# Who empties the first keys' bank, and when, in the first steps of an attention and feed-forward kernel

## The chip, the cores and the metric

One core of a Trainium2 chip runs one program. TensorE (PE) multiplies and transposes, VectorE (DVE) and ScalarE (ACT) work on what it leaves in its accumulator banks, GpSimd (POOL) works on on-chip memory, and SyncE (SP) issues the transfers. The metric is the device time of one execution in microseconds, as the median of several runs.

## The reference

Three blocks in a row: causal attention with a cumulative bias, a gated feed-forward block, and a mixing block.

```python
def _attn_ref(q, k, v, s):                       # (4, 8, 576, 64), s: (4, 8, 576)
    scores = (1 / np.sqrt(D)) * np.matmul(q, k.transpose(0, 1, 3, 2))
    cum = np.cumsum(np.maximum(s, 0.0), axis=-1)
    bias = -(cum[:, :, :, None] - cum[:, :, None, :])
    scores = np.where(causal, -1000000000.0, scores + np.minimum(bias, 0.0))
    scores = scores - np.max(scores, axis=-1, keepdims=True)
    attn = np.exp(scores)
    attn = attn / (np.sum(attn, axis=-1, keepdims=True) + 1e-09)
    return np.matmul(attn, v)
def _moe_ref(x, w_in, g_ln, w_sg, b_sg, w_out):  # x: (4, 576, 512)
    u, v = halves of gelu(x @ w_in)
    v_s = np.einsum('ts,bsd->btd', w_sg, layernorm(v) * g_ln) + b_sg[None, :, None]
    return x + (u * v_s) @ w_out
def _moe2_ref(x, w_theta, w_tok_r, w_tok_i, w_ch):
    theta = x @ w_theta
    u = x + einsum(w_tok_r, x * cos(theta)) + einsum(w_tok_i, x * sin(theta))
    return u + np.maximum(u @ w_ch, 0.0)
```

## The kernel before

**Tiling.** Attention is done for 16 pairs of heads (4 batches of 4 pairs), each pair stacked to 128 partitions. A pair's 576 queries are five tiles `t` = 0 to 4, and a tile's causal row of exponentials is 64, 192, 320, 448 or 576 keys wide. The exponentials of both heads (`j` = 0, 1) lie in one tile `E`. For the value product they must be turned, keys onto partitions: 128x128 transposes (L465) write them to accumulator banks `T`, and an eviction brings each bank to on-chip memory. The banks have four kinds. Kind a holds the last keys (two blocks of one head, and for the second head also the 64 first keys of tile 0), kind b four blocks that go to `Ef[:, 512:1024]`, kind c four that go to `Ef[:, 0:512]`, and kind d the four blocks of the *first keys* of both heads, which go to `E0[:, 0:512]`. Kinds a and c are emptied by ScalarE (L477, L481, L483), kinds b and d by VectorE (L475, L479).

**The value product** (`values`) accumulates in two banks, Y and Z. Its calls are in this order: two over E0 (the first keys), two over `Ef` 0:512, two of 384 columns, two of 128, two of 256 columns over the last keys, and two over the 64 first keys of tile 0 into Z. VectorE multiplies the result by the reciprocal sums (L536, L537) and `finish_pair` makes the high and low halves `x` for the feed-forward block. The reciprocal sums `r` of a pair are turned by one transpose (`turned`, L490) into a part of a bank, copied to `rT` by ScalarE (L492), stored, and loaded again, spread over partitions, as `xT` (`load_r`, L509).

**Banks.** Scores use four accumulator banks. A pool of two banks holds Y, Z and, outside the cases below, every T; a second pool of two holds the feed-forward accumulators `fo` and, in the first steps, the banks of kinds b and d and that of the sums' transpose. A bank is written again only when its eviction has been done.

**Order.** Attention begins with hand-written steps p = 1 to 4 (`first_steps`, `FIXED` = 5), whose instructions stand on each engine in the order in which they are written. Step p does, for pair p: scores of tiles 4, 1, 0, then of 3, 2; `reduced` (VectorE, L424: bias, mask and the row's extreme); `expo` (ScalarE, L435: exponentials and their sums); `inverse` (VectorE, L440 and L441: the reciprocals). In the same step it does the value product of pair p-2, with the sums' transpose of pair g = p-1 in its midst (the argument `between` of `values`), and the transposes of pair g, whose evictions are written between the reductions and exponentials. Beside these, VectorE, ScalarE and POOL prepare a feed-forward weight (`bits`: L744, L745, L749; `part32`: the cast to `wih` at L104 and the low half `wil` at L112).

After step 4 come the value product of pair 3 and the loop of `attention`, p = 5 to 16. There scores, transposes (`transpose_units`) and value products of three pairs are units of a string, and between units feed-forward products fill TensorE by a plan; a scheduler then sets the order of the instructions. `transpose_units` gives the kinds in the order c0, b0, a0, c1, b1, a1, d.

Of the kernel before, what the change touches and what calls it, by code (L numbers as in the profile page):

```python
# [55 lines left out]
class Kernel:  # L56
# [396 lines left out]
    def transposes(self, pr, kind, j, pool=None):  # L453

        nc = self.nc
        E, E0 = self.Es[pr], self.E0[pr % 2]
        blocks = {"a": [(0, 3, 3), (128, 4, 3)] + ([(256, 0, 0)] if j else []),
                  "b": [(QS[t] - 192, t, 2) for t in range(2, 5)] + [(384, 4, 4)],
                  "c": [(QS[t] - 64, t, 1) for t in range(1, 5)],
                  "d": [(QS[t] - 64, t, 0) for t in range(1, 5)]}[kind]  # L460
        T = self.psF.tile([P, 512], F32, name="T", tag="fo") if pool else self.psT.tile(
            [P, 512], F32, name="T", tag="T")
        for col, t, kt in blocks:
            c = EOFF[t] + QE[t] - 64 if kt == 0 else EOFF[t] + (QE[t] + QS[kt] if j else QE[t] - QE[kt])
            nc.tensor.transpose(T[:, col:col + P], E[:, c:c + P], self.ident)  # L465
        if kind == "a" and not j and not pool and pr not in self.turns:
            self.turned(pr, T)
        if kind != "d":
            Ef = self.Efs.get((pr, j))
            if Ef is None:  # L470
                Ef = self.Efs[pr, j] = self.a2.tile([P, 1280], F32, name="Ef", tag="Ef", bufs=3)

        def away():
            if kind == "b":
                nc.vector.tensor_copy(Ef[:, 512:1024], T)  # L475
            elif kind == "c":
                nc.scalar.copy(Ef[:, 0:512], T)  # L477
            elif kind == "d":
                nc.vector.tensor_copy(E0[:, 0:512], T)  # L479
            else:  # L480
                nc.scalar.copy(Ef[:, 1024:1280], T[:, 0:256])  # L481
                if j:
                    nc.scalar.copy(E0[:, 512:576], T[:, 256:320])  # L483
        return away
# [12 lines left out]
        self.ET[pr] = (self.E0[pr % 2], [self.Efs.pop((pr, j)) for j in (0, 1)])  # L497

    def transpose_units(self, pr):
        for kind, j, cost in (("c", 0, 440.0), ("b", 0, 440.0), ("a", 0, 330.0), ("c", 1, 440.0),  # L500
                              ("b", 1, 440.0), ("a", 1, 330.0), ("d", 1, 440.0)):
            self.transposes(pr, kind, j)()
            yield cost
        self.transposed(pr)
# [6 lines left out]
    def values(self, pr, between=None):  # L511

        nc = self.nc
        E0, Efs = self.ET.pop(pr)
        v0, vr = self.vop.pop(pr)
        Y = self.psT.tile([P, 512], F32, name="Y", tag="T")
        Z = self.psT.tile([P, 512], F32, name="Z", tag="T")[:, 0:64]

        calls = []
        halves = [slice(i * D, i * D + D) for i in (0, 1)]  # L520
        for js in halves:
            calls.append((Y[js], v0[:, js], E0[:, 0:512], True, False))
        for kt, a, c, n in ((1, 0, 0, 512), (2, 128, 512, 384), (4, 384, 896, 128), (3, 256, 1024, 256)):
            for js, F in zip(halves, Efs):
                calls.append((Y[js, a:a + n], vr[:, kt - 1, js], F[:, c:c + n], False, kt == 3))
        for js in halves:
            calls.append((Z[js], v0[:, js], E0[:, 512:576], True, True))
        if between:
            self.row(calls[0:4])
            between()  # L530
            calls = calls[4:]
        self.row(calls)

        def away(eng="act"):
            xT = self.xTs.pop(pr)
            nc.vector.tensor_tensor(xT[:, 512:576], Z, xT[:, 512:576], op=ALU.mult)  # L536
            nc.vector.tensor_tensor(xT[:, 0:512], Y, xT[:, 0:512], op=ALU.mult)  # L537
            self.finish_pair(pr, xT, eng)
        return away
# [41 lines left out]
    def first_steps(self):  # L581

        self.load_cum(1)
        self.load_piece(1)
        self.load_v(0)
        self.scale(0)
        self.scores(0, 1)
        self.spin(self.psT.tile([P, 512], F32, name="spin", tag="T"), 8)
        for t in (3, 2):
            self.reduced(0, (t,))  # L590
            self.expo(0, (t,))
        del self.cums[0]
        self.bits(0)
        self.inverse(0)
        self.high(2)
        self.scale(1)

        room = self.f1.tile([P, 5 * FH], F32, name="room", tag="vT")
        self.load_cum(2)
        self.load_pair(3, at=room[:, 0:2 * S])  # L600
        for p in range(1, self.FIXED):
            g = p - 1
            self.scores(p, 0)
            if p == 1:
                self.turned(g, self.psF.tile([P, 512], F32, name="T", tag="fo"))
                self.load_pair(4, "K")
                self.load_piece(2)
            else:
                self.load_cum(p + 1)
                self.load_piece(p + 1)  # L610
                if p == 2:
                    self.load_pair(5, at=room[:, 2 * S:4 * S])
                elif p == 3:
                    self.load_pair(6, "K")
            self.reduced(p, (1, 0, 4), (0,))
            if p == 1:
                self.expo(p, (1, 0, 4), (0,))
                a0 = self.transposes(g, "a", 0)
                c0 = self.transposes(g, "c", 0)
                b0 = self.transposes(g, "b", 0, True)  # L620
                self.part32(g)
                self.reduced(p, (1, 0, 4), (1,))
                a0()
                c0()
                self.expo(p, (1, 0, 4), (1,))
                b0()
                self.load_r(g)
                self.scores(p, 1)
            else:
                self.scale(p)  # L630
                away = self.values(
                    p - 2, lambda: self.turned(g, self.psF.tile([P, 512], F32, name="T", tag="fo")))
                self.part32(g)
                self.expo(p, (1, 0, 4), (0,))
                self.reduced(p, (1, 0, 4), (1,))
                self.expo(p, (1, 0, 4), (1,))
                self.low_q(p + 1, self.raw.pop(("Q", p + 1)))
                if p == 3:
                    self.load_pair(6, "Q")
                self.scores(p, 1)  # L640
                away("pool")
                self.load_r(g)
                self.load_v(p)
                a0 = self.transposes(g, "a", 0)
                b0 = self.transposes(g, "b", 0, True)
                c0 = self.transposes(g, "c", 0)
            b1 = self.transposes(g, "b", 1, True)
            self.reduced(p, (3,))
            if p == 1:
                self.expo(p, (3,))  # L650
                self.low_q(p + 1, self.raw.pop(("Q", p + 1)))
                self.load_pair(4, "Q")
                self.load_v(p)
            else:
                a0()
                self.expo(p, (3,), (0,))
                c0()
                self.expo(p, (3,), (1,))
                b0()
            if p + 2 <= self.FIXED:  # L660
                self.high(p + 2)
            a1 = self.transposes(g, "a", 1)
            a1()
            self.reduced(p, (2,))
            del self.cums[p]
            d = self.transposes(g, "d", 1, True)
            c1 = self.transposes(g, "c", 1)
            if p < self.FIXED - 1:
                self.expo(p, (2,), (0,))
                c1()  # L670
            else:
                c1()
                self.expo(p, (2,), (0,))
            self.expo(p, (2,), (1,))
            b1()
            d()
            self.transposed(g)
            if p < self.FIXED - 1:
                self.bits(p, lambda: self.inverse(p))
            else:  # L680
                self.inverse(p)
                self.bits(p)
                self.load_piece(p + 2)
        self.part32(self.FIXED - 1)
        queued = next(i for i in reversed(self.nc.cur_bb.bb.instructions) if i.engine == mybir.EngineType.SP)
        self.values(self.FIXED - 2)("act")
        return queued
# [688 lines left out]
```

## Time and profile before

| | before |
|---|---|
| median of 3 runs | 635.86 us (635.04 to 636.33) |
| profiled execution | 635.9 us, of which span 634.2 us |
| TensorE's granted clock in it | 0.999 of full speed |
| TensorE busy | 98% of the span |
| VectorE / ScalarE / POOL busy | 68% / 55% / 27% |

A row of a timeline gives the start in us from the span's start, the length in us, the engine, the line, the operation with its output and input, the count of such instructions, and in square brackets the idle time before it with what released it. Neighbouring instructions overlap, so an engine goes on a little before the length of a row is over. The kernel counts its steps from 1; step 3 lies at 34.58 to 45.08 us by TensorE's scores, step 4 at 45.08 to 56.

### The profile page before, as it was taken

The numbers are of one execution on the slowest core, as the hardware profiler recorded it, in microseconds if no ns is written. First come the engines' busy times: TensorE is split into PE (matmuls) and PEld (weight loads), VectorE is DVE, ScalarE is ACT, GpSimd is POOL, SyncE is SP. The second block draws the span as 40 slices with busy tenths as digits, with TensorE's granted clock in tenths as the row PEclk, the third lists the DMA queues.
The fourth block names the chain that finished last, engine by engine and source line by source line (L and its number), as shares of the span: only waits on it lengthen the run. The fifth ranks groups of instructions, "written<-read, shape, count | busy, mean of one in ns | idle before, by whom it ended". The sixth has DMA issues, their size and how long they took to land.

```text
span 634.2 us, 12664 instructions
## 1 busy us (share of the span) xinstructions
PE 618.7 (98%) x4703; PEld 542.1 (85%) x4703; DVE 429.6 (68%) x1051; ACT 348.6 (55%) x808; POOL 172.2 (27%) x199
## 2 busy tenths in 40 slices
PE   8999998999999999999999999999999999999997
PEld 6676777887787788778799998899999899999997
DVE  7898678556787786888386367878654674578222
ACT  6886788756779555884265145646432561465000
POOL 6464524433043431134446554000001000100000
PEclk9999999999999999999999999999999999999999
DMA  6876772776564756336468696320013001200101
GB/s 186 273 241 209 234 214 83 221 232 224 163 186 155 244 201 199 115 93 227 161 212 250 201 328 220 111 77 20 1 38 114 1 1 57 94 0 2 75 1 75
DMA packets 54878, 90.98 MB, mean 143 GB/s; under 512 B 8640, under 2 KB 22560, under 8 KB 54816
## 3 DMA queue, kind: packets, MB, share of 16 engines
q1 hardware_dynamic: 54816, 90.17, 44.2%
q8 instruction: 37, 0.61, 0.4%
q14 instruction: 25, 0.20, 0.1%
HBM read 65.32 MB, written 24.83 MB: 142 GB/s over the span
## 4 chain that ended last, share of the span: by engine, by line
PE 67%; DVE 6%; ACT 4%; DMA 3%; POOL 2%; issue 1%; SPq 0%; DVEq 0%; ACTq 0%; POOLq 0%
PE yo L115 18%; PE fo L115 18%; PE co L115 8%; PE th L115 7%; PE wo L115 5%; PE Y L115 4%; PE T L465 3%; PE sc L115 3%; DMA x2d<-xr 1%; POOL vT L941 1%; PE tp L1092 1%; ACT E L435 1%; DMA wd<-wtabs 1%; DMA x2T<-x2d 1%; DVE stats L1015 1%
## 5 line engine op out<-in xcount | busy, mean ns | idle before, releaser
L435 ACT ACTIVATE E<-E,negm 128x192 f32<-128x192 f32 (+4 forms) x160 | 88.3, 554 | 6.3 <-DVE negm L424 6.0
L115 PE MATMUL yo<-wkl,zh 128*128 128x288 f32 x288 | 85.5, 297 | 0.0
L115 PE MATMUL yo<-wkh,zl 128*128 128x288 f32 x288 | 85.4, 297 | 0.0
L115 PE MATMUL yo<-wkh,zh 128*128 128x288 f32 x288 | 84.8, 296 | 0.0
L424 DVE CUSTOM_DVE_ANT_0 E<-sc,C 128x192 f32<-128x192 f32 (+4 forms) x160 | 69.0, 485 | 2.6 <-PE sc L115 1.8
L465 PE MATMUL T<-ident,E 128*128 128x128 f32 x400 | 57.0, 276 | 3.2 <-DVE xT L537 1.2
L115 PE MATMUL fo<-x,wih 128*128 128x288 f32 x256 | 56.3, 303 | 1.9 <-ACT uT L1012 1.9
L115 PEld LDWEIGHTS yo<-wkl,zh 128*128 128x128 f32 x288 | 54.1, 188 | 0.6
L115 PEld LDWEIGHTS yo<-wkh,zh 128*128 128x128 f32 x288 | 53.9, 188 | 0.5
L115 PEld LDWEIGHTS yo<-wkh,zl 128*128 128x128 f32 x288 | 54.0, 188 | 0.4
L465 PEld LDWEIGHTS T<-ident,E 128*128 128x128 f32 x400 | 45.7, 140 | 7.5 <-DVE Ef L475 2.1
L115 PEld LDWEIGHTS fo<-x,wih 128*128 128x128 f32 x256 | 41.8, 188 | 4.8 <-ACT uT L1012 3.0
L108 POOL TENSOR_SCALAR xt<-x2s 128x128 fp32r<-128x128 f32 x8 | 4.0, 494 | 148.7 <-DVE x2s L112 147.9
L115 PE MATMUL fo<-wih,x 128*128 128x512 f32 x128 | 42.7, 403 | 0.0
L115 PE MATMUL sc<-kh,qh 64*128 64x288 f32 (+1 forms) x192 | 39.1, 365 | 1.4 <-DVE negm L424 1.1
L1049 POOL TENSOR_TENSOR uT<-gt,uT 128x288 f32<-128x288 f32 x32 | 26.4, 830 | 51.7 <-DVE gt L1047 45.3
L115 PE MATMUL fo<-wsh,vh 128*128 128x288 f32 x128 | 38.7, 306 | 1.0 <-DVE gt L1047 1.0
L115 PE MATMUL wo<-gh,woh 128*128 128x288 f32 x128 | 38.3, 300 | 0.4 <-DVE xr L1068 0.4
L115 PE MATMUL fo<-x,wil 128*128 128x288 f32 x128 | 38.4, 303 | 0.0
L115 PE MATMUL Y<-Ef,vr 128*64 128x512 f32 (+3 forms) x256 | 38.1, 434 | 0.0
L115 PE MATMUL fo<-wsl,vh 128*128 128x288 f32 x128 | 37.9, 299 | 0.0
L115 PE MATMUL fo<-wsh,vl 128*128 128x288 f32 x128 | 37.8, 298 | 0.0
(228 smaller groups left out, 1763.5 us busy)
## 6 DMA issues: line engine op xcount, KB each, us to landing
C<-cd SPq DMA_DIRECT2D x15, 576.0 KB, 5.3
xT<-rd SPq DMA_DIRECT2D x32, 144.0 KB, 3.3
xd<-xT SPq DMA_DIRECT2D x16, 288.0 KB, 4.9
gd<-uT SPq DMA_DIRECT2D x16, 288.0 KB, 3.0
gr<-gd SPq DMA_DIRECT2D x16, 288.0 KB, 4.5
xr<-xd SPq DMA_DIRECT2D x16, 288.0 KB, 4.5
x2d<-xr SPq DMA_DIRECT2D x16, 288.0 KB, 2.5
x2T<-x2d SPq DMA_DIRECT2D x16, 288.0 KB, 4.1
```

The costliest lines, as they stand in the source:

```text
L108: nc.gpsimd.tensor_scalar(out, src, 1.0, 1.0, op0=ALU.mult, op1=ALU.mult)
L115: return self.nc.tensor.matmul(out, lhsT, rhs, start=start, stop=stop)
L424: self.nc.vector.tensor_tensor_reduce(at if j else at[:, ::-1], self.sc[t, j].rearrange("p (b k) -> p b k", k=64), C[:, j, 0:n].rearrange( ...
L435: self.nc.scalar.activation(at, at, AF.Exp, bias=self.negm[pr % 2][:, j, c:c + 1], scale=-1.0, accum_out=sm[:, j * 5 + c:j * 5 + c + 1])
L465: nc.tensor.transpose(T[:, col:col + P], E[:, c:c + P], self.ident)
L941: (nc.vector if alone else nc.gpsimd).tensor_scalar(vT[0:r, t], vT[0:r, t], rs[0:r, t:t + 1], nm[0:r, t:t + 1], op0=ALU.mult, op1=ALU.add)
L1015: nc.vector.bn_stats(stats[:, t], vT[:, t])
L1049: nc.gpsimd.tensor_tensor(uT[:, ft, a:a + m], gt, uT[:, ft, a:a + m], op=ALU.mult)
L1092: nc.tensor.transpose(tp[0:r, dt * P:(dt + 1) * P], x2T[:, dt, a:a + r], self.ident)
```

## The change

Four edits.

1. In steps 2 and 3 kind d (the first keys) is emptied by ScalarE, written after both exponentials of tile 2. In steps 1 and 4 VectorE still empties it.
2. In `values` the sums' transpose stands behind six calls (E0, `Ef` 0:512, 384 columns) and no longer behind four. This touches the three value products of steps 2 to 4.
3. In step 4, b0 is emptied before the reductions of tile 3, and then the order is a1, c1, d, b1, the reductions of tile 2, the exponentials of tile 2. Before it was a1, the reductions of tile 2, c1, the exponentials, b1, d.
4. In the loop, `transpose_units` gives c0, b0, a0, d, c1, b1, a1.

```diff
-        def away():
+        def away(eng="dve"):
...
             elif kind == "d":
-                nc.vector.tensor_copy(E0[:, 0:512], T)
+                self.rnd(eng, E0[:, 0:512], T)
...
-        for kind, j, cost in (("c", 0, 440.0), ("b", 0, 440.0), ("a", 0, 330.0), ("c", 1, 440.0),
-                              ("b", 1, 440.0), ("a", 1, 330.0), ("d", 1, 440.0)):
+        for kind, j, cost in (("c", 0, 440.0), ("b", 0, 440.0), ("a", 0, 330.0), ("d", 1, 440.0),
+                              ("c", 1, 440.0), ("b", 1, 440.0), ("a", 1, 330.0)):
...
         if between:
-            self.row(calls[0:4])
+            self.row(calls[0:6])
             between()
-            calls = calls[4:]
+            calls = calls[6:]
...
             b1 = self.transposes(g, "b", 1, True)
+            last = p == self.FIXED - 1
+            if last:
+                b0()
             self.reduced(p, (3,))
...
                 self.expo(p, (3,), (1,))
-                b0()
+                if not last:
+                    b0()
...
             a1()
-            self.reduced(p, (2,))
-            del self.cums[p]
+            if not last:
+                self.reduced(p, (2,))
             d = self.transposes(g, "d", 1, True)
             c1 = self.transposes(g, "c", 1)
-            if p < self.FIXED - 1:
+            if not last:
                 self.expo(p, (2,), (0,))
                 c1()
+                self.expo(p, (2,), (1,))
+                b1()
+                d("act" if p > 1 else "dve")
             else:
+
                 c1()
-                self.expo(p, (2,), (0,))
-            self.expo(p, (2,), (1,))
-            b1()
-            d()
+                d()
+                b1()
+                self.reduced(p, (2,))
+                self.expo(p, (2,))
+            del self.cums[p]
```

ScalarE at the end of step 2 and the start of step 3, before and then after (L477 empties kind c, L435 are the exponentials, L492 the sums; the copy by `rnd` has line L104):

```order
L435 ACTIVATE E,sm_81<-E,negm_79 128x320
L477 COPY Ef<-T 128x512
L435 ACTIVATE E,sm_81<-E,negm_79 128x320
L492 COPY rT<-T 10x128
L104 CAST wih<-wtab 128x512
```

```order
L435 ACTIVATE E,sm_81<-E,negm_79 128x320
L477 COPY Ef<-T 128x512
L435 ACTIVATE E,sm_81<-E,negm_79 128x320
L104 COPY E_75<-T 128x512
L492 COPY rT<-T 10x128
L104 CAST wih<-wtab 128x512
```

The first keys' copy has come between the last exponential of the step and the next step's sums; the same piece stands once more between steps 3 and 4.

VectorE in step 4, as one piece of the difference (L536 and L537 multiply the value product, L424 are the reductions, L475 empties kind b, the copy by `rnd` has line L106):

```order
 L536 TENSOR_TENSOR xT<-Z,xT 128x64
 L537 TENSOR_TENSOR xT<-Y,xT 128x512
+L475 COPY Ef<-T 128x512
 L424 ISA E,negm_79<-sc,C 128x7x64
 L424 ISA negm_79 128x1
 L424 ISA E,negm_79<-sc,C 128x448
 L424 ISA negm_79 128x1
+L106 COPY E_75<-T 128x512
 L475 COPY Ef<-T 128x512
 L424 ISA E,negm_79<-sc,C 128x5x64
```

One eviction of kind b has moved ahead of tile 3's reductions, and the first keys' copy has moved from the step's end to the place behind them.

VectorE in the last round of the loop, around the transposes of the last pair, before and then after (lines after the edit are 9 higher here: L749 is L758, L1047 is L1056):

```order
L744 TENSOR_SCALAR wtabs<-wtabs 128x288
L745 SCALAR_TENSOR_TENSOR wtabs<-wroom,wtabs 128x288
L749 SCALAR_TENSOR_TENSOR wtabs<-wroom,wtabs 128x288
L1047 SCALAR_TENSOR_TENSOR gt<-fo,gcol,bsg 128x288
L479 COPY E_75<-T 128x512
L537 TENSOR_TENSOR xT<-Y,xT 128x512
```

```order
L753 TENSOR_SCALAR wtabs<-wtabs 128x288
L754 SCALAR_TENSOR_TENSOR wtabs<-wroom,wtabs 128x288
L758 SCALAR_TENSOR_TENSOR wtabs<-wroom,wtabs 128x288
L1056 SCALAR_TENSOR_TENSOR gt<-fo,gcol,bsg 128x288
L475 COPY Ef<-T 128x512
L537 TENSOR_TENSOR xT<-Y,xT 128x512
```

The last eviction ahead of the value product's multiply was that of the first keys; it is now that of kind b of the second head. On TensorE seven transposes in a row stand directly ahead of this last value product in both kernels: a1 and d before, b1 and a1 after.

## Rows read from the trace of the kernel before

**Rows 1.** The page, part 1: busy us, share of the span, instructions of each engine.

```profile
PE 618.7 (98%) x4703; PEld 542.1 (85%) x4703; DVE 429.6 (68%) x1051; ACT 348.6 (55%) x808; POOL 172.2 (27%) x199
```

**Rows 2.** Busy time by stretch: length, PE, PEld, DVE, ACT, POOL, clock, DMA, GB/s.

```profile
34.58:45.08 10.50, 10.29 (x106) 7.34 (x106) 10.43 (x32) 8.49 (x29) 6.51 (x8) 1.00 0.67 227
...
92.00:112.00 20.00, 18.23 (x157) 14.68 (x157) 17.48 (x48) 17.71 (x49) 10.43 (x10) 1.00 0.39 108
...
175.00:212.00 37.00, 34.72 (x297) 29.80 (x296) 30.68 (x88) 28.92 (x69) 14.41 (x16) 1.00 0.55 173
```

**Rows 3.** Timeline of VectorE, steps 3 and 4.

```profile
34.83 0.68 DVE L479 COPY E<-T 128x512 f32<-128x512 f32 x1
35.43 1.33 DVE L744 TENSOR_SCALAR wtab<-wtab 128x512 uint32<-128x512 uint32 x1
...
52.86 0.62 DVE L424 CUSTOM_DVE_ANT_0 E<-sc,C 128x448 f32<-128x448 f32 x1
...
55.97 0.69 DVE L479 COPY E<-T 128x512 f32<-128x512 f32 x1
...
57.88 0.36 DVE L744 TENSOR_SCALAR wtab<-wtab 128x512 uint32<-128x512 uint32 x1
```

**Rows 4.** Timeline of TensorE, steps 2 and 3.

```profile
27.72 0.33 PE L490 MATMUL T<-ident,r 128*128 128x128 f32 x1 [0.15 <-DVE r L441]
...
36.53 1.08 PE L115 MATMUL Y<-E,v 128*64 128x512 f32 x4
...
38.66 1.52 PE L115 MATMUL Y<-Ef,vr 128*64 128x384 f32 x12
...
44.05 1.09 PE L465 MATMUL T<-ident,E 128*128 128x128 f32 x8 [0.21 <-DVE Ef L475]
```

**Rows 5.** Timeline of ScalarE, steps 2 to 4.

```profile
36.60 0.20 ACT L435 ACTIVATION_READ_ACCUMULATOR E<-E,negm 128x1 f32 x1
38.81 0.25 ACT L492 COPY rT<-T 10x128 f32<-10x128 f32 x1 [2.01 <-PE T L490]
...
43.55 0.57 ACT L477 COPY Ef<-T 128x512 f32<-128x512 f32 x1
...
47.10 0.21 ACT L435 ACTIVATION_READ_ACCUMULATOR E<-E,negm 128x1 f32 x1
49.31 0.25 ACT L492 COPY rT<-T 10x128 f32<-10x128 f32 x1 [2.00 <-PE T L490]
...
53.52 0.67 ACT L435 ACTIVATE E<-E,negm 128x448 f32<-128x448 f32 x1
...
55.57 0.22 ACT L483 COPY E<-T 128x64 f32<-128x64 f32 x1
```

**Rows 6.** Timeline of TensorE, step 4 and the product after it.

```profile
47.03 1.08 PE L115 MATMUL Y<-E,v 128*64 128x512 f32 x4
...
52.41 2.08 PE L465 MATMUL T<-ident,E 128*128 128x128 f32 x17
...
56.76 1.08 PE L115 MATMUL Y<-E,v 128*64 128x512 f32 x4 [0.97 <-ACT Ef L477]
```

**Rows 7.** Timelines of SyncE's queue and VectorE after step 4.

```profile
57.47 1.10 SPq L509 DMA_DIRECT2D xT<-rd  x2
...
61.01 0.23 DVE L536 TENSOR_TENSOR xT<-Z,xT 128x64 f32<-128x64 f32 x1 [1.32 <-DMA xT<-rd]
```

**Rows 8.** Timelines of ScalarE, VectorE and TensorE at the last pair's product.

```profile
307.42 0.22 ACT L483 COPY E<-T 128x64 f32<-128x64 f32 x1
...
307.59 0.69 DVE L479 COPY E<-T 128x512 f32<-128x512 f32 x1
...
308.38 1.08 PE L115 MATMUL Y<-E,v 128*64 128x512 f32 x4 [0.83 <-ACT E L483]
```

**Rows 9.** Timeline of TensorE in the loop, at its longest wait there.

```profile
95.92 0.77 PE L465 MATMUL T<-ident,E 128*128 128x128 f32 x5 [0.96 <-DVE xT L537]
```

## The prediction, made before the changed kernel ran

> **What bounds the kernel now.** I read the page first, for the busy shares. TensorE is busy 618.7 us, 98% of the span [rows 1], so a change gains where TensorE waits and loses where it is made to wait. The profiled execution took 635.9 us, 634.2 of it span, against a median of 635.86 for the runs shown. I sum against 635.9.
>
> Then the busy time by stretch. In step 3 (34.58 to 45.08, 10.50 us) VectorE is busy 10.43, TensorE 10.29, ScalarE only 8.49 [rows 2]. VectorE looks like the bound, and its copy of the first keys' bank takes 0.68 [rows 3]. Whether TensorE pays for that copy stands in TensorE's own timeline [rows 4]. The value product over the first keys starts at 36.53 with no wait noted, a microsecond after that copy ended at 35.51. The one wait of the step is 0.21, before the last eight transposes, on a copy of *another* bank (L475). So TensorE gives back at most 0.21 per step if VectorE gets lighter.
>
> ScalarE's timeline is a strict queue [rows 5]: the copy of the transposed sums (rT), a weight cast, ten exponentials with evictions between them, then rT of the next step. In step 3 rT starts at 38.81, the last read of an exponential at 47.10, and then ScalarE waits 2.00 for the sums' transpose of step 4. That looks like slack, but it lies *between* two things that the change ties together.
>
> **The first keys' bank on ScalarE (steps 2 and 3).** VectorE loses one copy of 0.68 per step; ScalarE gets one of 128x512, which takes 0.57 there [rows 5]. Its place decides: it is queued behind the last exponential of its step. Step 2's last read starts at 36.60 and lets go of the engine about 0.10 later, so the copy runs from 36.70 to 37.27, where VectorE's ended at 35.51. The product over the first keys in step 3 then starts at about 37.35 instead of 36.53: +0.8. Nothing covers that: TensorE's order is written by hand here, and the scores ahead of the product are done.
>
> **The sums' transpose two calls later.** It moves behind the products of 384 columns. The twelve instructions of L115 after it took 1.52 [rows 4]; half their columns belong to the moved calls, and half of 1.52 less the overlap at its end is about 0.66. No work is added; only rT comes later. In step 2 the transpose waits 0.15 for the reciprocals as it stands [rows 4], so part of the move is free there, and ScalarE's small waits on VectorE take up more: I take 0 (bounds 0 and 0.66). In steps 3 and 4 all of it counts, since ScalarE is idle until rT.
>
> **The cycle that these two make.** Step 3: product at 37.35, rT 2.28 behind it as before (38.81 less 36.53) plus 0.66, so at 40.29. ScalarE is busy without a gap from rT to 0.09 after the last read starts (38.81 to 47.19, 8.38). So step 3's copy runs from 48.67 to 49.24 and the product of step 4 starts at 49.32, where it was 47.03 [rows 6]: +2.3. Its rT comes 2.94 later, at 52.26 instead of 49.31. Per step the loop through ScalarE is 8.38 + 0.57 + 0.08 + 2.94 = 12.0 us, against the 10.50 that TensorE and VectorE need. The slack of 2.00 is smaller than what is hung into it.
>
> **The last step (4).** VectorE keeps the first keys' copy here, but earlier. Before, TensorE waits 0.97 for the product at 56.76; the row names ScalarE, but VectorE's copy runs from 55.97 to 56.66 [rows 3, 6] and is the later one. Moving it ahead takes that wait away. On the other side the first bank (b0) is now copied ahead of the reductions of 448. Transposes start 5.38 after the product (52.41 less 47.03), so at 54.70. Six of the 17, which took 2.08 together, are written at 55.45; the copy, at 0.60 apart from the next (35.43 less 34.83), ends at 56.1. The reduction of 0.62 with its read [rows 3] gives its result at 56.75. ScalarE's exponential of 448 began 4.21 after rT (53.52 less 49.31), which would be 56.47; it waits until 56.75. The copy that frees the product's accumulator bank (L483) ended 2.27 after that exponential began (55.57 and 0.22), so now at 59.0, and the product starts at 59.1: **+2.3**. In other words 2.94 of lateness in rT and 0.3 from b0, less 0.97. Bounds: +0.8 if the last step's order recovers all but the first wait, +2.9 if it recovers nothing of rT's lateness.
>
> What else is queued: VectorE multiplies this value product after the weight bits of the last step, near 63. Before, L536 waited 1.32 at 61.01 for a load of the sums, which SP issues at 57.47 behind a store of an earlier tile [rows 7]; that store follows a multiply of step 4 that comes about 1 us later, so the load lands by 62, before VectorE gets there. POOL's low halves for the first feed-forward products come about 2.3 later, as TensorE does. I put 0 for these (0 to +0.3).
>
> VectorE's next instruction, a shift on 128x512, took 1.33 in step 3 and 0.36 at the end of step 4 [rows 3]. Freed of the copy it may start earlier and run shorter, up to 1.0 in each step. What TensorE could take of that (0.21) now lies beside the wait for ScalarE, so 0.
>
> **First keys' transposes fourth (planned loop, 12 steps).** Most transposes there lie between feed-forward products that cover the evictions. Where they don't is the last pair of heads: the seven last transposes are followed by the value product at 308.38 with 0.83 of wait noted. ScalarE's copy (L483) begins at 307.42 and takes 0.22; VectorE's copy of the first keys runs from 307.59 for 0.69, to 308.28 [rows 8], and is what the product needs. In the new order that bank is empty long before, which would give up to -0.9. But only two banks turn. The last seven are now b1 and a1, the product's accumulator takes the older of the two, b1's, and VectorE copies b1 behind the same gate multiply, in the place that the first keys had. It still ends near 308.28: **0** (bounds 0 and -0.9).
>
> In the rest of the loop TensorE is idle 1.77 us in 92 to 112 and 2.28 in 175 to 212 [rows 2]. The costliest wait there, 0.96 at 95.92, is for a value accumulator's eviction on VectorE [rows 9]. The scheduler has re-ordered feed-forward products, evictions and reductions around all of these. I followed the first stretch by hand: that wait stays, a later one for a transposes' bank goes, a new one for the gate's operand comes: -0.4, with an error as large. For the second I take 0, with half its idle time either way, +-1.1.
>
> **Sum.** +2.3 + 0 - 0.4 = +1.9, so 635.9 + 1.9 = **637.8**. Its own range is 636.6 to 639.0.
>
> **Rivals.** (a) *Not slower: the last step recovers it.* If b0's bank, and so the reductions, come sooner than I reckon and the product waits for neither, the lateness at the loop's start is only the first wait, +0.8: 635.9 + 0.8 - 0.4 = 636.3. Against: it is ScalarE's queue, not VectorE's, that holds the accumulator's bank.
>
> (b) *Not slower: the loop gives it back.* The product's first operand is ready three groups earlier in every step. If half of the 1.77 and 2.28 goes (2.0) and the last pair gives its 0.9: 635.9 + 2.3 - 0.9 - 2.0 = 635.3. It decides if the accumulator takes a bank that ScalarE frees. Against: the waits I could name are on other banks.
>
> (c) *Faster: VectorE sets the pace of the first steps.* It is busy 10.43 of 10.50 [rows 2]. If ScalarE's wait of 2.00 is free room after all, two copies of 0.68 come off: 635.9 - 1.4 - 0.4 = 634.1. Against: TensorE's rows show no wait on the moved copy. The Trainium skill ("Perfetto Trace Analysis", section "Optimizing Scalar/DVE Operations") says that with a saturated DVE moving some operations to Scalar may make sense; this trace agrees that VectorE is saturated in these steps, and by that rule this would be the outcome.
>
> (d) *Slower still: an eviction in the middle.* In the loop the first keys' bank now has to come back through VectorE before a later group can be written. Where VectorE is in a row of gate multiplies or statistics, that group waits, as at 95.92. It shows from the first such wait on; with two, 2 x 0.96 on the sum gives 639.7. Against: feed-forward products stand between the groups.
>
> **How the numbers follow.** Forecast 0.50, (a) 0.12, (b) 0.16, (c) 0.10, (d) 0.12. A measurement of this kernel tells about 0.2% (1.3 us) from no change, so faster is below 634.6 and slower above 637.2. Of the forecast 0.42 lies above and 0.08 within; (a) gives 0.10 within and 0.02 above; (b) 0.10 within and 0.06 below; (c) is faster, (d) slower. That is faster 0.16, same 0.28, slower 0.56. The range leaves out most of (c), the faster part of (b), and the upper half of (d): 634.9 to 639.6.
>
> **What the profile after would show.** Right: in steps 3 and 4 the product over the first keys waits for ScalarE's copy, at about 37.35 and 49.3; ScalarE's wait before rT grows from 2.0 to about 3.0; step 4's rT comes near 52.3; the last hand-written product starts at 59.1; in the last pair the product still waits some 0.8 after the seven transposes. Wrong: products at 36.5 and 47.0 as before, or steps shorter than 10.5; a last product near 57.6, which is (a); no wait in the last pair, which is (b); new waits of TensorE on evictions in the loop, which is (d).

## The result, and the profile after

The changed kernel takes 641.05 us (median of 6 runs, 639.74 to 642.42) against 636.05 us for the kernel before in the same sessions (6 runs, 635.04 to 636.33). The ratio is 1.0081, with a 95% interval of 1.0065 to 1.0096: about 5 us slower. The forecast was slower by 1.9, with a range up to 639.6, so the sign is right and the size is wrong.

In the profiled execution the span is 638.5 us, where it was 634.2. TensorE executes as many instructions as before and is busy 619.6 us, where [rows 1] has 618.7. So 0.9 of the 4.3 us that the span is longer is busy time, and the rest is waiting:

```profile
PE 619.6 (97%) x4703; PEld 543.0 (85%) x4703; DVE 423.3 (66%) x1049; ACT 350.0 (55%) x810; POOL 171.9 (27%) x199
```

I cut the span at three marks that don't depend on where a trace sets its zero: the first call of the first value product, the first feed-forward product after the hand-written steps, and the last call of the last value product that goes into Y.

| | first steps | planned loop | the rest, to the end |
|---|---|---|---|
| before | 36.93 | 248.84 | 322.95 |
| after | 39.22 (+2.29) | 250.67 (+1.83) | 323.31 (+0.36) |

So there are two places.

**The first steps.** TensorE's timeline of the changed kernel in steps 3, 4 and behind (compare [rows 4, 6]):

```profile
37.34 1.08 PE L115 MATMUL Y<-E,v 128*64 128x512 f32 x4 [0.73 <-ACT E L104]
...
49.19 1.08 PE L115 MATMUL Y<-E,v 128*64 128x512 f32 x4 [1.04 <-ACT E L104]
...
57.82 0.66 PE L465 MATMUL T<-ident,E 128*128 128x128 f32 x4 [0.57 <-ACT Ef L477]
58.85 1.08 PE L115 MATMUL Y<-E,v 128*64 128x512 f32 x4 [0.38 <-ACT E L483]
```

Both products that need the first keys now wait for ScalarE's copy (L104), and the last one starts at 58.85, where it was 56.76. ScalarE's timeline shows the cycle (compare [rows 5]):

```profile
36.70 0.58 ACT L104 COPY E<-T 128x512 f32<-128x512 f32 x1
40.26 0.26 ACT L492 COPY rT<-T 10x128 f32<-10x128 f32 x1 [2.98 <-PE T L490]
...
48.58 0.56 ACT L104 COPY E<-T 128x512 f32<-128x512 f32 x1
52.11 0.26 ACT L492 COPY rT<-T 10x128 f32<-10x128 f32 x1 [2.98 <-issue]
...
56.53 0.67 ACT L435 ACTIVATE E<-E,negm 128x448 f32<-128x448 f32 x1 [0.32 <-DVE negm L424]
```

The two rT stand 11.85 us apart, where they stood 10.50 apart, and ScalarE waits 2.98 for each.

**The loop.** One wait stands out that the kernel before doesn't have, of TensorE at the accumulator Z of pair 9's value product:

```profile
201.89 0.29 PE L115 MATMUL sc<-kh,ql 64*128 64x288 f32 x1
204.38 0.33 PE L115 MATMUL Z<-E,v 128*64 128x64 f32 x2 [2.20 <-ACT Ef L481]
```

Z takes a bank that held two transposed blocks and the turned sums of pair 10. ScalarE empties it with L492 and L481, and its timeline tells why so late (L1032 is the second half of the feed-forward block's activation, which needs a table loaded before and another one after it):

```profile
197.22 1.28 ACT L1032 ACT_TABLE_LOAD   x1
198.51 2.13 ACT L1032 ACTIVATE uT<-uT 128x2304 f32<-128x2304 f32 x1
200.55 0.65 ACT L104 CAST kh<-K 128x576 fp32r<-128x576 f32 x1
201.22 1.28 ACT L435 ACT_TABLE_LOAD   x1
...
203.83 0.24 ACT L492 COPY rT<-T 10x128 f32<-10x128 f32 x1
203.97 0.36 ACT L481 COPY Ef<-T 128x256 f32<-128x256 f32 x1
```

The last of the transposes and the turned sums are written at 195.75 to 196.18, and the two copies come some 8 us later, behind all of that. In the kernel before the same copies ran ahead of the activation:

```profile
196.07 0.36 ACT L481 COPY Ef<-T 128x256 f32<-128x256 f32 x1
...
200.00 2.13 ACT L1023 ACTIVATE uT<-uT 128x2304 f32<-128x2304 f32 x1
```

The wait has an aftermath. Busy time by stretch of the changed kernel (length, PE, PEld, DVE, ACT, POOL, granted clock, DMA, GB/s):

```profile
202.00:204.30 2.30, 0.18 (x3) 0.00 (x0) 0.00 (x0) 2.29 (x8) 1.33 (x2) 1.00 0.55 142
204.30:206.00 1.70, 1.62 (x19) 1.29 (x19) 1.27 (x4) 1.48 (x6) 0.00 (x0) 1.00 0.34 37
206.00:209.60 3.60, 3.60 (x21) 3.55 (x18) 1.88 (x7) 1.01 (x2) 1.96 (x3) 0.54 1.00 366
209.60:212.00 2.40, 2.40 (x20) 2.40 (x19) 1.66 (x4) 0.61 (x2) 1.34 (x2) 0.97 0.94 275
```

From 206 to 209.6 TensorE is granted about half its clock, the lower of its two levels (1.2 GHz), though it is busy throughout. 3.60 us at 0.54 hold 1.94 us of work at full clock, so this costs 1.7 more at most. It is a bound, since waits that TensorE would otherwise have had there can vanish in a slower stretch.

**The last pair** still waits, as reckoned, for b1's bank on VectorE (compare [rows 8]): 1.13, where it was 0.83.

```profile
312.29 1.08 PE L115 MATMUL Y<-E,v 128*64 128x512 f32 x4 [1.13 <-DVE Ef L475]
```

### The profile page after: what moved, and what is told of

Its sections match the earlier page's. It is cut to its first block, busy times and chain, and to the rows that moved or that the text cites. A ratio compares the mean times of both kernels' runs of the same rounds, so it can differ in the third digit from the quotient of the medians.

```text
span 638.5 us, 12677 instructions
## 1 busy us (share of the span) xinstructions
PE 619.6 (97%) x4703; PEld 543.0 (85%) x4703; DVE 423.3 (66%) x1049; ACT 350.0 (55%) x810; POOL 171.9 (27%) x199
## 4 chain that ended last, share of the span: by engine, by line
PE 68%; DVE 5%; ACT 4%; DMA 3%; POOL 2%; issue 1%; SPq 0%; DVEq 0%; POOLq 0%; ACTq 0%
PE fo L115 18%; PE yo L115 18%; PE co L115 8%; PE th L115 7%; PE wo L115 5%; PE Y L115 4%; PE T L465 3%; PE sc L115 3%; POOL vT L950 2%; ACT E L435 1%; PE tp L1101 1%; DMA x2T<-x2d 1%; DMA x2d<-xr 1%; DVE gl L112 1%; ACT vT L998 1%
## 5 line engine op out<-in xcount | busy, mean ns | idle before, releaser
L435 ACT ACTIVATE E<-E,negm 128x192 f32<-128x192 f32 (+4 forms) x160 | 88.2, 554 | 1.6 <-DVE negm L424 1.5
L424 DVE CUSTOM_DVE_ANT_0 E<-sc,C 128x192 f32<-128x192 f32 (+4 forms) x160 | 69.1, 484 | 5.7 <-PE sc L115 3.0
L1058 POOL TENSOR_TENSOR uT<-gt,uT 128x288 f32<-128x288 f32 x32 | 27.7, 867 | 50.3 <-DVE gt L1056 47.7
```

The source lines that it names most:

```text
L424: self.nc.vector.tensor_tensor_reduce(at if j else at[:, ::-1], self.sc[t, j].rearrange("p (b k) -> p b k", k=64), C[:, j, 0:n].rearrange( ...
L435: self.nc.scalar.activation(at, at, AF.Exp, bias=self.negm[pr % 2][:, j, c:c + 1], scale=-1.0, accum_out=sm[:, j * 5 + c:j * 5 + c + 1])
L1058: nc.gpsimd.tensor_tensor(uT[:, ft, a:a + m], gt, uT[:, ft, a:a + m], op=ALU.mult)
```

## The experiments

The theory after this reading: two losses that have nothing to do with each other, 2.3 us in the first steps by edits 1 to 3, and some 2.7 in the loop by edit 4 (5.0 by the medians less 2.3; the profiled execution, one of the faster, has 1.83 there), there through one bank behind ScalarE's activation and the low clock that follows. The rivals are in each expectation. Every kernel was compared with the kernel before on the same chip; "steps" and "loop" are the marks of the table above, from one profile each. Three kernels with the first steps of the kernel before gave 36.73 to 36.77 for the steps, where the table has 36.93, so 0.2 there is noise.

### Edits 1 to 3, without the loop's order

```diff
-        for ... ("a", 0, 330.0), ("d", 1, 440.0), ("c", 1, 440.0), ("b", 1, 440.0), ("a", 1, 330.0)
+        for ... ("a", 0, 330.0), ("c", 1, 440.0), ("b", 1, 440.0), ("a", 1, 330.0), ("d", 1, 440.0)
```

> Edits 1 to 3 of the change, with the loop's order of the kernel before (c0 b0 a0 c1 b1 a1 d). Theory: the loss has two separate halves, one in the first steps and one in the loop. By the changed kernel's trace the first steps cost 2.1 to 2.35 us (last hand-written product at 58.85 instead of 56.76, first feed-forward product at 64.74 instead of 62.39), so 636.05 + 2.3 = 638.3, and no wait of 2 us at Z near 204. Rival: the loop's loss comes from its late start, which shifts work against transfers; then this kernel loses all 5 and takes 641.

638.65 us against 636.55, ratio 1.0033 (1.002 to 1.0046). Steps 39.25, loop 248.84, to the hundredth that of the kernel before, and no wait at Z. The late start of 2.3 us changes nothing in the loop; the rival falls.

### Edit 4 alone

The same diff the other way round, on the kernel before.

> Edit 4 alone: first keys' transposes fourth in the loop, first steps as before. Theory of two halves: 5.0 - 2.3 = 2.7 lost, 638.8, with the wait of about 2.2 us for the bank that ScalarE empties behind the table loads and the long gelu (product accumulator Z, some 2.3 us earlier than 204), and TensorE at half its clock for about 3 us after it. Rival (late start): no loss, 636.

638.88 us against 636.55, ratio 1.0042 (1.0028 to 1.0057). Steps 36.73, loop 250.27 (+1.43). The wait is there with the same 2.20, and the low clock behind it:

```profile
202.36 0.33 PE L115 MATMUL Z<-E,v 128*64 128x64 f32 x2 [2.20 <-ACT Ef L481]
```

```profile
204.00:205.00 1.00, 1.00 (x11) 0.94 (x10) 0.74 (x5) 0.23 (x1) 0.00 (x0) 0.50 0.95 359
205.00:206.00 1.00, 1.00 (x6) 1.00 (x5) 0.39 (x1) 0.44 (x1) 0.47 (x1) 0.50 1.02 371
```

The two halves, 2.1 and 2.3, add up to 4.4 of the 5.0; the missing 0.6 is within their intervals.

### The changed kernel without the wait at Z

```diff
+            elif pr == 10 and not j:
+                nc.vector.tensor_copy(Ef[:, 1024:1280], T[:, 0:256])
             else:
                 nc.scalar.copy(Ef[:, 1024:1280], T[:, 0:256])
...
-        nc.scalar.copy(rT, T[0:10, 256:384])
+        (nc.vector.tensor_copy if pr == 10 else nc.scalar.copy)(rT, T[0:10, 256:384])
```

> The changed kernel with one bank of the loop (kind a of the first head of pair 10, with its turned sums) emptied by VectorE and not by ScalarE. It takes away what makes Z wait at 204. Theory: the wait of 2.2 us goes, and with it the stretch at half clock (about 3.4 us at 0.50, so 1.7 us): 641.05 - 3.9 = 637.2, less if another wait takes its place. Rival: the low clock has another cause than that wait and stays: 638.9.

637.69 us against 636.55, ratio 1.0019 (1.0009 to 1.0028): 1.1 over before, as expected (637.2 against 636.05). Steps 39.26, loop 248.00: 2.67 shorter than the changed kernel's and 0.84 shorter than that of the kernel before. The wait is gone, and the clock stays up over the same place:

```profile
205.00:206.00 1.00, 0.38 (x3) 0.39 (x4) 0.73 (x4) 0.64 (x3) 0.00 (x0) 1.00 0.54 108
206.00:207.00 1.00, 1.00 (x10) 1.00 (x9) 0.75 (x2) 0.96 (x3) 0.65 (x1) 1.00 1.00 389
```

Another wait has moved in, 0.83 for VectorE's multiply at 205.62, and the clock stays at 1.00 behind it. So both the wait and the low clock hang on that one bank, and with this bank moved edit 4 no longer lengthens the loop but shortens it.

### The changed kernel with VectorE copying in steps 2 and 3

```diff
-                d("act" if p > 1 else "dve")
+                d()
```

> The changed kernel with the first keys' bank emptied by VectorE in steps 2 and 3 again (edits 2, 3, 4 stay). Theory: the place of that copy in ScalarE's queue is what costs in the first steps, since the slack of 2.0 us there holds the later sums' transpose alone (0.66): product at 36.5 and 47.0 again, last hand-written product near 56.9, so 641.05 - 2.2 = 638.8. Rival: the later transpose alone is to blame: then still over 640.

640.28 us against 636.55, ratio 1.0057 (1.004 to 1.0074): +3.7, where I expected +2.75 (638.8 against 636.05). Two things were wrong with the expectation. Steps are 38.26, still 1.33 over before: the products start 11.13 apart and not 10.50. And the low clock lasted longer here, from 204 to past 210, after a wait of the same length (2.19):

```profile
204.00:205.00 1.00, 0.76 (x3) 0.57 (x3) 0.42 (x2) 1.00 (x5) 0.00 (x0) 0.50 0.03 5
...
209.00:210.00 1.00, 1.00 (x6) 0.98 (x5) 0.29 (x1) 0.00 (x0) 0.82 (x2) 0.50 0.99 320
```

This makes the loop 252.13, 1.46 longer than the changed kernel's. So the rival's number (over 640) came, but the later transpose is only in part its cause: with VectorE copying 1.33 of the 2.29 us in the steps remain. To see whose they are, edits 1 to 3 were run one by one.

### Edit 1 alone

```diff
... (the eviction takes its engine as an argument, as in the change)
-            d()
+            d("act" if 1 < p < self.FIXED - 1 else "dve")
```

> Edit 1 alone on the kernel before: steps 2 and 3 empty the first keys' bank on ScalarE, behind the last exponential; the sums' transpose stays behind four calls, last step and loop as before. Theory (place in ScalarE's queue): the loop through ScalarE is 8.38 + 0.57 + 0.08 + 2.28 = 11.3 us against 10.5; product of step 3 at 37.35, of step 4 at 48.7, last one 1.6 late: +1.6 on before. Rival (VectorE's 0.6 us per step is what counts): faster than before by up to 0.4.

637.68 us against 636.40, ratio 1.0015 (1.0004 to 1.0027). Steps 38.30 (+1.37), a little under the +1.6 expected. The products stand where the queue puts them, 11.29 apart, and TensorE's only other wait between them is the 0.21 for VectorE that it had before:

```profile
37.39 1.08 PE L115 MATMUL Y<-E,v 128*64 128x512 f32 x4 [0.76 <-ACT E L104]
...
48.68 1.08 PE L115 MATMUL Y<-E,v 128*64 128x512 f32 x4 [0.76 <-ACT E L104]
```

### Edit 2 alone

```diff
-            self.row(calls[0:4])
+            self.row(calls[0:6])
```

> Edit 2 alone: the sums' transpose behind six calls. Theory by the run with VectorE copying in steps 2 and 3: ScalarE's weight cast comes 0.66 later, POOL's low half with it, and this then lies beside VectorE's multiply-subtract of step 3 and 4 (L571, 0.75 alone, 1.38 and 1.25 beside it), which pushes VectorE, the busiest engine here, by some 0.5 per step: +1.1 on before. Rival: ScalarE's slack of 2.0 us takes the move up: no change.

637.25 us against 636.40, ratio 1.0015 (1.0004 to 1.0027). Steps 38.12 (+1.19). The rows of VectorE, POOL and TensorE in step 3 (L571 makes the low half of a later pair's queries, L112 is POOL's subtraction for the weight):

```profile
40.54 1.38 DVE L571 SCALAR_TENSOR_TENSOR ql<-Q,qh 128x576 fp32r<-128x576 f32 x1
```

```profile
40.01 1.28 POOL L112 TENSOR_TENSOR wil<-wtab,wih 128x512 fp32r<-128x512 f32 x1 [3.01 <-ACT wih L104]
```

```profile
42.10 2.08 PE L465 MATMUL T<-ident,E 128*128 128x128 f32 x17 [0.55 <-DVE xT L536]
```

In the kernel before, POOL's subtraction is nearly over when L571 starts:

```profile
39.66 1.30 POOL L112 TENSOR_TENSOR wil<-wtab,wih 128x512 fp32r<-128x512 f32 x1 [2.38 <-ACT wih L104]
```

```profile
40.83 0.75 DVE L571 SCALAR_TENSOR_TENSOR ql<-Q,qh 128x576 fp32r<-128x576 f32 x1
```

With the sums' transpose later, ScalarE's weight cast and POOL's subtraction behind it come later too and lie across L571, which ends 0.63 after POOL does (41.29) instead of 0.75 after its own start. VectorE is the busiest engine here, the multiplies of the value product (L536, L537) are next in its queue, and the transposes wait for the banks that they free. From the start of the product over the first keys to L536 it is 5.61 us, where it was 4.97, and to the transposes 5.87, where it was 5.24. So ScalarE's slack does take up the later transpose, and the cost comes on two other engines. This is read from the rows; no run kept POOL's subtraction in its old place. (With edit 1 alone L571 is held too, to 1.70 us, but there it starts earlier after the product, and L536 follows the product by 4.96 as before.)

### Edit 3 alone

The changed kernel with edits 1, 2 and 4 undone; the main part of what is left of the change, in step 4:

```diff
+            if last:
+                b0()
             self.reduced(p, (3,))
...
                 c1()
-                self.expo(p, (2,), (0,))
-            self.expo(p, (2,), (1,))
-            b1()
-            d()
+                d()
+                b1()
+                self.reduced(p, (2,))
+                self.expo(p, (2,))
```

> Edit 3 alone: the last step's order. Theory: the exponential of tile 3 now waits for b0's copy and the reductions behind it (about 1 us), as much as the first keys' wait gives back (0.97): within 0.3 of before. Rival: the wait of 0.97 goes and nothing comes for it: -0.9.

636.16 us against 636.40, ratio 1.0000 (0.9987 to 1.0013). Steps 37.22 (+0.29), but that lies ahead of step 4, which alone edit 3 touches: from step 4's product to the end of the steps it is 15.39, where it was 15.36. The waits of 0.21 (before the last eight transposes) and 0.97 (at the product) are gone, and about as much has come in two others:

```profile
56.19 0.66 PE L465 MATMUL T<-ident,E 128*128 128x128 f32 x4 [0.95 <-ACT Ef L477]
57.22 1.08 PE L115 MATMUL Y<-E,v 128*64 128x512 f32 x4 [0.38 <-ACT E L483]
```

### The copy on ScalarE, but ahead of the exponentials

```diff
... (the eviction takes its engine as an argument, as in the change)
+            if 1 < p < self.FIXED - 1:
+                d("act")
             if p < self.FIXED - 1:
                 self.expo(p, (2,), (0,))
                 c1()
...
-            d()
+            if not 1 < p < self.FIXED - 1:
+                d()
```

> As edit 1 alone, but the copy stands ahead of tile 2's exponentials in ScalarE's queue and not behind them. Theory: only the place costs. Step 3's copy then ends 1.1 us earlier than with edit 1, the product needs no wait, ScalarE's slack shrinks from 2.0 to 1.4, and VectorE has 0.6 us less in two steps: the 0.21 waits for its evictions may go, -0.4 to 0 on before. Rival (any such copy on ScalarE costs): +0.6 or more.

636.19 us against 636.40, ratio 1.0000 (0.9987 to 1.0013). Neither product of steps 3 and 4 waits, and they stand 10.47 apart:

```profile
37.47 1.08 PE L115 MATMUL Y<-E,v 128*64 128x512 f32 x4
...
44.98 1.09 PE L465 MATMUL T<-ident,E 128*128 128x128 f32 x8 [0.21 <-DVE Ef L475]
47.94 1.08 PE L115 MATMUL Y<-E,v 128*64 128x512 f32 x4
```

With edit 1 it was 11.29. The same copy on the same engine costs 0.8 per step in one place of the queue and nothing in the other. And 0.6 us less work per step on VectorE, 99% busy there, buys 0.03 per step at most: the wait of 0.21 stays.

### The changed kernel with four calls again

```diff
-            self.row(calls[0:6])
+            self.row(calls[0:4])
```

> The changed kernel with the sums' transpose behind four calls again (edits 1, 3, 4 stay). Theory: the loop through ScalarE is 11.3 us per step and not 11.9, so step 4's sums come 1.3 us earlier than in the changed kernel; the last step's order, which makes the exponential wait for b0, gives part of it back: 0.6 to 1.2 less than the changed kernel, +3.4 to +4.2 on before.

640.41 us against 636.73, ratio 1.0051 (1.0033 to 1.0068): +3.7 by the medians, +3.2 by the ratio. The products of steps 3 and 4 start at 36.74 and 48.03, 11.29 apart like with edit 1 alone; steps are 38.68 (+1.75). The loop is 251.65, and its low clock was again a long one, behind the same wait:

```profile
203.24 0.48 PE L115 MATMUL Z<-E,v 128*64 128x64 f32 x2 [2.18 <-ACT Ef L481]
```

```profile
203.00:204.00 1.00, 0.76 (x3) 0.57 (x3) 0.42 (x2) 1.00 (x5) 0.00 (x0) 0.50 0.03 5
...
208.00:209.00 1.00, 1.00 (x6) 0.98 (x5) 0.29 (x1) 0.00 (x0) 0.83 (x2) 0.50 1.01 332
```

### Towards a faster kernel

First edit 4 on the kernel before, with pair 10's bank emptied by VectorE (the diff shown above):

> The kernel before with edit 4 alone (first keys' transposes fourth), and the one bank of pair 10 with its turned sums emptied by VectorE, as in the run that took away the wait at Z. Theory: apart from that wait edit 4 gains: the run with edit 4 alone reached the product of pair 5 0.9 us earlier than the kernel before, and the run without the wait lost nothing more between there and the end: -0.7 on before. Rival: edit 4 is worth nothing outside that wait: no change.

635.40 us against 636.73, ratio 0.9978 (0.9966 to 0.9990). Loop 248.30, 0.54 shorter than before. The kernel before with this bank moved and without edit 4 was not run, so it is not shown how the gain divides between the two. Then also the last pair's b1 on ScalarE:

```diff
             if kind == "b":
-                nc.vector.tensor_copy(Ef[:, 512:1024], T)
+                (nc.scalar.copy if pr == 15 and j else nc.vector.tensor_copy)(Ef[:, 512:1024], T)
```

> As the run before it, and the last pair's bank b1 is emptied by ScalarE, which is idle there, instead of by VectorE behind a gate multiply. Theory: the last value product waits for b1's bank, whose copy runs on VectorE in the place that the first keys' copy had; on ScalarE it starts as soon as it is written and the wait of 0.8 shrinks to about 0.2: another -0.5, so -1.2 on before. Rival: the product waits for another bank or operand: no difference to the run before it.

635.14 us, ratio 0.9965 (0.9950 to 0.9980). Loop 247.59. The wait of the last product, in the run before it and in this one:

```profile
307.04 1.08 PE L115 MATMUL Y<-E,v 128*64 128x512 f32 x4 [0.77 <-DVE Ef L475]
```

```profile
306.66 1.08 PE L115 MATMUL Y<-E,v 128*64 128x512 f32 x4 [0.35 <-ACT Ef L475]
```

That it shrinks when b1's copy moves shows that the product does wait for b1's bank. That this kernel is faster than the one without the move isn't shown, since their intervals overlap. At last also the early copy on ScalarE in steps 2 and 3 (its diff is shown above):

> As the run before it, and the first keys' copy of steps 2 and 3 on ScalarE ahead of tile 2's exponentials. Theory: that early copy gained 0.03 us per step in its trace, so -1.2 to -1.3 on before, no difference to the run before it that can be told.

634.51 us against 636.73, ratio 0.9956 (0.9939 to 0.9972): 2 to 3 us faster than the kernel before, and by the two ratios (0.9956 and 1.0081) some 8 faster than the changed one. Loop 247.77, steps 36.66. That this run is faster than the one before it isn't shown, since their intervals overlap.

## Why the prediction was right and wrong

**The cycle through ScalarE: right.** Reckoned were products at 37.35 and 49.32, rT at 40.29 and 52.26, the exponential of the last step at 56.75, the last product at 59.1. The trace has 37.34 and 49.19, 40.26 and 52.11, 56.53, and 58.85. Part of that closeness is luck, since the two traces reach the first mark 0.21 apart; counted from it, the first of these products is 1.0 late, where 0.8 was reckoned. The term +2.3 measured +2.29 in the profile and +2.1 in the times of edits 1 to 3 alone. The run with the copy ahead of the exponentials shows that it is the place in the queue, as argued. It answers rival (c) too: VectorE, though saturated, was relieved of the same two copies, and nothing came of it (ratio 1.0000).

**What edit 2 does: half right.** Inside that cycle its 0.66 counts nearly as reckoned: rT comes 2.92 behind the product (2.94 reckoned), and a step takes 11.85 with it and 11.29 without, 0.56 apart. In step 2, where I took 0, nothing can be told: from the first mark to the product of step 3 it is 12.08 us in the changed kernel and 12.04 with four calls again. But I looked only at ScalarE. By itself the edit costs about as much through POOL and VectorE (+1.19), which the text had not among its queues. In the changed kernel that clash isn't there, since L571 starts ahead of POOL's subtraction, which starts at 41.12 and takes 1.47:

```profile
40.68 0.75 DVE L571 SCALAR_TENSOR_TENSOR ql<-Q,qh 128x576 fp32r<-128x576 f32 x1
```

So the parts measured alone (1.37 and 1.19) need not add up to the whole (2.29). That the clash left the changed kernel alone was luck, since the text had not looked for it.

**The last step: right.** The relief is eaten by b0's copy ahead of the reductions: alone, edit 3 moves nothing that can be told (0.03 in its stretch).

**The last pair: right.** No gain, for the reason given (b1's bank).

**The rest of the loop: wrong.** This is the step that failed: "-0.4" for the first stretch and "0, +-1.1" for the second. In the stretch of 92 to 112 I expected 0.4 less idle time and it is nearly the same: 1.73 of 20 us, where it was 1.77. In the stretch of 175 to 212 I took the waits that were there and let them shrink or grow by half. They did shrink: between 165 and 215 the waits noted are 2.3 us in all before, and 0.4 besides the one at Z with edit 4 alone. One of them is gone with edit 4. It was the longest wait of the loop before, and not the 0.96 of [rows 9]:

```profile
207.87 0.40 PE L115 MATMUL fo<-wsh,vh 128*128 128x288 f32 x1 [1.02 <-DVE gt L1047]
```

The loss came as a wait that was not there before, 2.20 us at Z: a bank whose evictions the scheduler had now put behind a table load and a long activation. I had read the order of TensorE and VectorE around such places and not ScalarE's, though all that was needed could be seen in the order: the copies of pair 10's bank behind the activation, and Z next in that bank. With the activation (2.13), two table loads (1.28 each) and the work between them behind it, the wait could have been bounded. Rival (d) had a new wait in the loop, but on VectorE, and at 0.96 each.

Then the low clock was missing in my sum altogether: no row of the kernel before shows it in the loop. With both, edit 4 costs 2.3 by its own run (+1.43 in the profiled execution), and with that bank on VectorE it gains 1.3 (0.6 to 2.2 by the interval).

**Spread.** The changed kernel's six runs have a mean clock of 0.997 or 0.995 of full speed: three at 639.74 to 640.75 with the first, three at 641.35 to 642.42 with the second. That fits a low stretch of one length or another behind the same wait, as the profiles of the four kernels with this wait have it (some 3.4 us in two, 6.8 in two). It isn't proof: single runs of kernels without that wait have 0.995 to 0.997 too (636.37 of the kernel before, 639.33 with edit 3 alone), and no trace of them shows where.

## What to carry to other kernels

Idle time of an engine with a fixed queue is only free if neither what it waits for nor what waits for it lies in the same loop: add up the loop from product to sums to queue end and back, and compare it with the period, before putting anything at the queue's end. Where a scheduler orders the work, look at the bank whose eviction stands behind the longest thing on its engine (a table load with its activation), and ask who writes that bank next. And a wait of TensorE of 2 us may cost more than its length: without the one of 2.20 at Z the loop was 2.67 shorter, although a wait of 0.83 had come in its place.

## What the hardware showed

TensorE's granted clock fell to half (0.50) at one wait of 2.2 us in a loop that was otherwise full. In the changed kernel it fell 1.9 us after TensorE had started again (204.38 to 206.3), with edit 4 alone 1.1 us after (202.36 to 203.4), and in both it stayed low for some 3.4 us. In the runs with VectorE copying and with four calls again it fell before the wait was over (near 204.0, with TensorE starting again at 204.24, and near 202.4, with 203.24) and stayed low for some 6.8 us, although TensorE was busy. Waits of up to 1.30 us in the loops (that one with edit 4 and pair 10's bank on VectorE, at 95.08) left it at 1.00. What sets the delay and the length was not tried.

VectorE's two-input instruction of 128x576 on on-chip memory took 0.75 us with POOL idle (before, at 30.32) and 1.38 when POOL's subtraction was already running, and it ended 0.63 after that one. Where it started first, it took 0.75 and the subtraction 1.47 instead of 1.28. The Trainium skill ("SBUF — State Buffer", section "SBUF: two separate sides") says that GpSimd and a VectorE instruction with two such inputs share a port pair, which the first one holds for its whole instruction while the other is blocked; the trace agrees.
